# Gating the first weight load on the first scaled q, with a new written order for the opening of a gated linear attention and MLP kernel

## The chip, the cores and the metric

The kernel runs on one core of a Trainium2 chip. The time is the device time of one execution in microseconds (us); lower is better. A profiled execution also has a span, from the first to the last instruction of the program; its own time is a little longer.

## The reference

Two parts follow each other. The first is a gated linear recurrence for 4 batches of 8 heads, 768 tokens, 48 values a head. The second is a two-layer MLP with a tanh gelu, on the 3072 tokens that the first part yields.

```
for t in range(768):                                   # per batch and head
    state = alpha[t][:, None] * state + outer(k[t], v[t])   # 48 x 48
    y[t]  = q[t] @ state
x   = y as (3072 tokens, 384)
out = gelu_tanh(x @ w_in) @ w_out                      # 384 -> 2048 -> 384
```

Inputs and outputs are float32; products inside are taken in bf16 (sums of logarithms in f16), with float32 sums.

## The kernel before

**Tiling.** Tokens are cut into 6 chunks of 128. A *pair* is one chunk of two batches, so there are 12 pairs, numbered 0 to 11; pairs 0 and 1 are the first chunk, pair 2 is the third pair. Within a pair, the two batches are units 0 and 1. The recurrence of a chunk is done in closed form: the logarithm of alpha (`ln`, line 349 or 351, ScalarE) is summed along the tokens by products on TensorE (`cum`, lines 336 to 370), its exponentials `b`, `binv` and `bend` come from ScalarE (lines 391 and 397), q is scaled by `b` and k by `binv` (`qp` and `kp`, line 408, VectorE; q' is the scaled q), both are transposed by TensorE (`t`, line 418) and copied out of PSUM (`ev`, line 436, ScalarE or VectorE), multiplied with each other (`attn`, line 479), masked to a triangle (`mask`, line 486, VectorE), and multiplied with v (`y`, lines 533 and 536). `x` copies the result out (line 543), `tx` transposes it (line 550) and `xe` copies the transpose (line 554). The state that goes on to the next chunk comes from `kv` (line 496) and `st` (lines 518 and 521). Pairs 0 and 1 are loaded in a packed layout, so their k is transposed back (`t`, line 444, and a further `ev`, line 451) before `kv`. `vb` casts v of these pairs (line 379).

**MLP.** `l1` (line 562) is one of 8 steps of layer one for a pair, 6 products of 128x256, `gelu` (line 568) its gelu on ScalarE, `l2` (line 581) one of 4 steps of layer two for one unit, 4 products of 128x384; `ot` (line 593) copies a result and a store sends it. W_in and W_out are loaded in 4 parts each. A step `l1` of number 0 or 1 needs part 0 of W_in, 2 or 3 part 1, and so on. Layer two of pairs 0 and 1 is one block of 16 steps (`l20.0` to `l20.15`) ordered by part of W_out. PSUM banks come from three rings: `ff` (4 banks: layer one and two, products on zeros, early sums), `yk` (2 banks: transposes, y, kv) and `ca` (double, for sums and attn).

**Order.** Nothing orders the engines but a list of tasks that a small planner in the kernel file makes (`Scheduler.order`, lines 64 to 162). It first follows a list written out by hand or by search, `FIRST` (lines 184 to 196), whose entries read engine:step, with P for TensorE, V for VectorE, A for ScalarE, G for GpSimd (called POOL in the profile), S for SyncE. A step's name is its kind, its pair (for `l1`, `gelu` and `l2` its block) and a number: `qp0.1` is the scaled q of pair 0, unit 1. `fill.3` means three products on zeros, which do no work of the kernel. When the list is used up, a greedy rule goes on, by costs in a table `W` and by deps and free buffers. Each engine executes its own tasks in that order; semaphores do the rest. `LANDED` (line 197) tells the planner when the first loads are there; no instruction comes from it.

**Loads.** The first twelve loads (alpha, q and k of pairs 0 and 1, each by unit) are issued by SyncE. All others are issued by GpSimd in the order of `LOADS` (line 179): `v0` and `v1` are v of pairs 0 and 1, `in 0` the first part of W_in, `out 0` the first part of W_out, `2a` and `2b` the units of pair 2, a bare number a whole pair. An entry `gate` makes GpSimd copy one column of a named tile (line 304), so that all that GpSimd issues afterwards is held until that tile is there. Loads by GpSimd cast to bf16 on the way, except v of pairs 0 and 1.

Of the kernel before, what the change touches and what calls it, by code (L numbers as in the profile page):

```python
# [21 lines left out]
COST = {  # L22
    ("ACT", "b"): (385, 135), ("ACT", "binv"): (385, 135), ("ACT", "ev"): (600, 40), ("ACT", "gelu"): (510, 110),
    ("ACT", "ln"): (430, 140), ("ACT", "vb"): (420, 140), ("ACT", "x"): (370, 140), ("DVE", "end"): (110, 90),
    ("DVE", "ev"): (605, 115), ("DVE", "kp"): (480, 120), ("DVE", "mask"): (605, 115), ("DVE", "qp"): (480, 120),
    ("DVE", "st"): (470, 130), ("DVE", "x"): (480, 120), ("DVE", "xe"): (270, 120),
}
LAT = {"SP": 0, "PE": 210, "ACT": 110, "DVE": 90, "POOL": 0}
# [18 lines left out]
class Scheduler:  # L47
# [16 lines left out]
    def order(self):  # L64
        free = {e: 0 for e in LAT}
        taken = {tag: [] for tag in self.bufs}
        table, wire, xbar, head, out = LN_EXP, 0, 0, 0, []
# [26 lines left out]
        def put(t, at, e):  # L94
            nonlocal wire, xbar
            for tag, users in t.takes:
                taken[tag].append(users)
            cost, lat = COST.get((e, t.kind), (t.cost[e], LAT[e])) if fixed else (t.cost[e], LAT[e])
            t.start, t.end, t.engine, t.load = at, at + cost, e, None
            free[e] = t.end  # L100
            t.done = t.end + lat
            if t.name in self.landed:
                t.done = self.landed[t.name]
                if e != "SP":
                    wire = t.done - W["receipt"]
            elif t.land is not None:
                wire = max(wire, t.end + W["lead"]) + t.land
                t.done = wire + W["receipt_hw" if e == "SP" else "receipt"]
            if t.kind in ("turn", "store"):
                xbar = t.done = max(xbar, t.end + W["landed"] - t.xbar) + t.xbar  # L110
                t.done += t.late
            out.append(t)

        def go(at, e, t):
            nonlocal table, head
            if e == "PE" and not fixed and self.fill and at < self.until and at - free[e] > 300:
                g = given("ff")
                n = int((at - max(free[e], g if g is not None else at) - 60) * 0.95 // W["fill"])
                if n > 0:
                    f = Task("fill", {"PE": n * W["fill"]}, 0, self.fill(n))  # L120
                    put(f.take("ff", f), max(free[e], g), e)
            put(t, at, e)
            if t.table not in (None, table):
                table = t.load = t.table
            for q in t.cost:
                left[q].remove(t)
            if t.stream is not None:
                head = min((x.stream for x in left["PE"] if x.stream is not None), default=None)

        fixed = True  # L130
        for step in self.first:
            e, name = step.split(":")
            if name[:5] == "fill.":
                n = int(name[5:])
                f = Task("fill", {"PE": n * W["fill"]}, 0, self.fill(n))
                at = given("ff")
                assert at is not None, "no bank for idle products"
                put(f.take("ff", f), max(free["PE"], at), "PE")
                continue
            e, t = {"P": "PE", "V": "DVE", "A": "ACT", "G": "POOL", "S": "SP"}[e], self.named[name]  # L140
            at = ready(t, False)
            assert at is not None, f"{name} can't go yet"
            go(max(at, free[e] + (W["table"] if t.table not in (None, table) else 0)), e, t)
        fixed = False
        while any(left.values()):
            best = None
            for e in LAT:
# [7 lines left out]
                if found:  # L155
                    window = min(f[2] for f in found) + 60
                    at, t, _ = min((f for f in found if f[2] <= window), key=lambda f: (f[1].prio, f[0]))
# [14 lines left out]
class _Kernel:  # L172
# [3 lines left out]

    SPLIT = (2,)
    EARLY = (0, 1)
    LOADS = ('gatea 0 1', 'v0', 'gateqp 0 1', 'in 0', 'v1', 'in 1', 'in 2', 'in 3', 'out 0', 'out 1', '2a', 'out 2', '2b', 'out 3', '3', '4', '5', '6', '7', '8', '9', '10', '11')

    PACKED, CUM_FF, R = (0, 1), (0, 1), 4
    RINGS = (('a', 0, 0, 1), ('a', 0, 1, 2), ('q', 0, 0, 1), ('k', 0, 0, 1), ('q', 0, 1, 2), ('k', 0, 1, 2),
             ('a', 1, 0, 1), ('a', 1, 1, 2), ('q', 1, 0, 1), ('k', 1, 0, 1), ('q', 1, 1, 2), ('k', 1, 1, 2))
    FIRST = """
        A:table.0 S:load.0 S:load.1 S:load.2 S:load.3 S:load.4 A:ln0.0 S:load.5 P:fill.7 P:cum0.0 A:ln0.1 G:gate.0 G:load.12 S:load.6 P:cum0.1 A:b0.0 S:load.7
        A:binv0.0 V:qp0.0 A:bend0.0 A:b0.1 V:kp0.0 S:load.8 P:fill.2 P:t0.0 A:bend0.1 A:binv0.1 V:ev0.0 P:t0.1 S:load.9 A:ev0.1 S:load.10 V:qp0.1 P:fill.3
        P:attn0.0 V:kp0.1 P:t0.2 G:gate.1 S:load.11 G:load.13 V:mask0.1 P:fill.1 P:t0.3 G:load.14 A:ev0.3 V:end0.0 V:ev0.2 A:ln1.0 V:mask0.0 P:fill.4
        P:attn0.1 G:load.15 P:cum1.0 V:mask0.2 A:vb0.0 G:load.16 A:ln1.1 V:vb0.1 P:y0.0 V:mask0.3 A:b1.0 P:cum1.1 G:load.17 A:x0.0 V:qp1.0 A:binv1.0 P:y0.1
        G:load.18 A:b1.1 P:t1.0 V:x0.1 A:bend1.0 G:load.19 A:ev1.0 V:kp1.0 P:fill.2 P:tx0.1 V:xe0.1 A:binv1.1 P:tx0.0 G:load.20 P:t1.1 A:bend1.1 V:xe0.0
        G:load.21 V:qp1.1 P:t0.5 A:ev1.1 V:kp1.1 G:load.22 A:ev0.5 P:fill.1 P:attn1.0 G:load.23 P:t1.3 V:mask1.1 P:t1.2 A:ev1.3 P:l10.0 G:load.24 V:mask1.0  # L190
        A:ev1.2 P:kv0.1 G:load.25 V:end1.0 V:st0.1 P:t0.4 G:load.26 P:attn1.1 A:ev0.4 P:t1.5 G:load.27 A:ev1.5 V:vb1.0 G:load.28 V:mask1.2 P:y1.0 P:l10.1
        G:load.29 A:x1.0 V:mask1.3 A:vb1.1 P:kv0.0 P:tx1.0 G:load.30 V:st0.0 P:l10.3 V:xe1.0 P:y1.1 P:kv1.1 G:load.31 P:l10.2 V:x1.1 A:gelu0.0 V:st1.1 P:tx1.1
        A:gelu0.1 G:load.32 P:l10.4 V:xe1.1 A:gelu0.3 P:l10.5 A:gelu0.2 G:load.33 P:l11.0 A:gelu0.4 A:gelu0.5 P:l11.1 A:gelu1.0 P:l11.2 A:gelu1.1 P:l11.6
        A:gelu1.2 P:l10.6 A:gelu1.6 P:l11.5 A:gelu0.6 P:l11.7 A:gelu1.5 P:l11.4 A:gelu1.7 P:l10.7 A:gelu1.4 P:l11.3 A:gelu0.7 P:t1.4 A:gelu1.3 P:l20.1 V:ev1.4
        P:l20.2 P:kv1.0 P:l20.5
    """.split()
    LANDED = {"load.0": 2800, "load.1": 3400, "load.2": 4400, "load.3": 5100, "load.4": 6750, "load.5": 7300, "load.12": 9850, "load.6": 9000, "load.7":
              10300, "load.8": 10800, "load.9": 11300, "load.10": 11900, "load.11": 12300, "load.13": 14900, "load.14": 17600, "load.15":
              19300, "load.16": 21300, "load.17": 23000, "load.18": 25000, "load.19": 26600, "load.20": 27700, "load.21": 28400, "load.22":
              29000, "load.23": 29400, "load.24": 31300, "load.25": 32100, "load.26": 32700, "load.27": 33300, "load.28": 33800, "load.29":  # L200
              35900, "load.30": 37700, "load.31": 39400, "load.32": 41300, "load.33": 42600}

# [399 lines left out]
    def tasks(self):  # L602
        s = self.s = Scheduler(self.BUFS, self.fill, 60000, self.FIRST, self.LANDED)
        B, NCH = self.B, self.NCH
# [28 lines left out]
        for r, m, lo, hi in self.RINGS:  # L633
            loads[r, m, lo] = loads[r, m, hi - 1] = s.add(
                "load", {"SP": W["ring_issue"]}, n, self.load(r, *pairs[m], lo, hi), land=(W["ring_v" if r == "v" else "ring"] * (hi - lo) // 2 if n else W["begin"]))
            n += 1
        for step in self.LOADS:
            if step[0] == "v":
# [261 lines left out]
```

## Time and profile before

| | us |
|---|---|
| median of 6 runs | 178.77 |
| lowest, highest | 177.92, 180.44 |
| the profiled execution | 179.0 |
| its span | 177.2 |
| TensorE busy in the span | 171.9 |
| ScalarE busy | 130.7 |
| VectorE busy | 94.9 |

In a timeline line the columns are: start in us, length in us, engine, line of the kernel, operation, output<-input by the program's names, shapes, and the number of instructions merged; in brackets the idle time of the engine ahead of it and what ended it. PE is TensorE, PEld its weight loads, DVE VectorE, ACT ScalarE. Ends of products are modelled, so two products that overlap in the list follow each other at the distance of their starts. Merged lines name the first shape only.

### The profile page before, as it was taken

The page shows a single profiled execution, that of the slowest core. Times are in us where ns is not written, and L with a number is a line of the kernel's source. Part 1 is how long each engine was busy: PE and PEld are TensorE (multiplying, and loading weights), DVE is VectorE, ACT ScalarE, POOL GpSimd, SP SyncE. Part 2 cuts the span into 40 slices and gives each one's busy share as a digit, 9 for nine tenths or more (in the row PEclk, how much of TensorE's full clock was granted, in tenths as well). Part 3 has the DMA queues.
Part 4 walks back from the last instruction along what each step waited for, and adds up shares of the span by engine and source line. Part 5 has one row for each costly group of instructions (what it writes and reads, how often), then busy time and mean ns, then how long its engine had stood idle before and what let it go on. Part 6 is the DMA issues. An engine that isn't in the chain of part 4 may idle for free.

```text
span 177.2 us, 4413 instructions
## 1 busy us (share of the span) xinstructions
PE 171.9 (97%) x1831; PEld 136.0 (77%) x1833; DVE 94.9 (54%) x187; ACT 130.7 (74%) x216; POOL 57.8 (33%) x64
## 2 busy tenths in 40 slices
PE   7999999999999999999999999999999999999992
PEld 2666899666896897797698698688697697786972
DVE  6498820454967994696499797495426505000000
ACT  4658899785898668858788967977988884481831
POOL 2387437996735766667640000000000000000000
PEclk9999999999999999999999999999999999999999
DMA  4999999999999999999999992361270360401102
GB/s 118 293 259 188 203 231 234 233 238 198 240 286 196 228 263 215 196 256 205 197 249 234 198 190 55 65 175 41 46 209 4 89 162 5 131 1 48 44 3 86
DMA packets 48900, 28.86 MB, mean 163 GB/s; under 512 B 37488, under 2 KB 45296, under 8 KB 48880
## 3 DMA queue, kind: packets, MB, share of 16 engines
q0 software_dynamic: 26464, 17.70, 60.8%
q1 hardware_dynamic: 22416, 10.88, 24.8%
q8 instruction: 14, 0.23, 0.6%
q14 instruction: 6, 0.05, 0.1%
HBM read 25.17 MB, written 4.72 MB: 169 GB/s over the span
## 4 chain that ended last, share of the span: by engine, by line
PE 89%; DMA 6%; ACT 2%; issue 1%; DVE 1%; SPq 0%; POOL 0%
PE hT L562 36%; PE acc L581 35%; DMA v<-in_v_dram 4%; PE at L479 4%; PE qkT_ps L418 3%; PE yps L536 3%; PE kv L496 2%; DMA a<-in_alpha_dram 2%; PE yps L533 2%; PE cum L368 2%; PE xT_ps L550 1%; ACT qkT L436 1%; PE cum L370 1%; PE k_ps L444 1%; PE cum L336 0%
## 5 line engine op out<-in xcount | busy, mean ns | idle before, releaser
L581 PE MATMUL acc<-w_out,gT 128*128 128x384 bf16 (+1 forms) x400 | 69.4, 319 | 0.0
L562 PE MATMUL hT<-xT,w_in 128*128 128x256 bf16 x576 | 68.8, 273 | 0.0
L568 ACT ACTIVATE gT<-hT 128x512 bf16<-128x512 f32 x96 | 56.1, 599 | 15.1 <-PE hT L562 11.6
L562 PEld LDWEIGHTS <-w_in 128*128 128x128 bf16 x576 | 61.2, 114 | 1.5
L581 PEld LDWEIGHTS <-gT 128*128 128x128 bf16 x400 | 36.5, 97 | 18.9
L486 DVE TENSOR_TENSOR atm<-at,ut 128x512 bf16<-128x512 f32 x48 | 30.1, 681 | 13.9 <-PE at L479 13.9
L408 DVE TENSOR_TENSOR qp<-q,b 128x768 bf16<-128x768 f32 (+1 forms) x15 | 11.9, 796 | 17.8 <-ACT b L397 17.8
L593 ACT COPY ot<-acc 128x384 f32<-128x384 f32 (+1 forms) x18 | 8.3, 461 | 13.7 <-PE acc L581 11.5
L298 POOL DMA_DIRECT2D k<-in_k_dram x11 | 12.2, 1108 | 8.8 <-DMA vb<-in_v_dram 3.7
L298 POOL DMA_DIRECT2D q<-in_q_dram x11 | 12.2, 1108 | 6.0 <-DMA w_in<-in_moe_w_in_dram 1.0
L298 POOL DMA_DIRECT2D a<-in_alpha_dram x11 | 12.2, 1113 | 5.4 <-DMA w_in<-in_moe_w_in_dram 1.3
L298 POOL DMA_DIRECT2D vb<-in_v_dram x11 | 12.1, 1103 | 5.1 <-DMA a<-in_alpha_dram 1.3
L270 ACT ACT_TABLE_LOAD x9 | 11.5, 1283 | 0.9 <-PEq L884 0.7
L397 ACT ACTIVATE b<-cum 128x768 bf16<-128x768 f32 (+1 forms) x15 | 10.2, 682 | 2.3 <-PE cum L370 1.5
L408 DVE TENSOR_TENSOR kp<-k,binv 128x768 bf16<-128x768 f32 (+1 forms) x15 | 11.8, 790 | 0.0
L568 ACT ACT_TABLE_LOAD x9 | 11.5, 1283 | 0.2
L397 ACT ACTIVATE binv<-cum 128x768 bf16<-128x768 f32 (+1 forms) x15 | 10.2, 681 | 0.0
L518 DVE TENSOR_TENSOR stmp<-kv,st 128x384 f32<-128x384 f32 x16 | 8.8, 552 | 2.0 <-PE kv L496 2.0
L543 DVE CAST x<-yps 128x384 bf16<-128x384 f32 x12 | 6.7, 557 | 5.6 <-PE yps L536 5.5
L521 DVE TENSOR_TENSOR st<-stmp,ends 128x384 bf16<-128x384 f32 x16 | 8.9, 558 | 0.6
L351 ACT ACTIVATE la<-a 128x768 f16<-128x768 f32 (+1 forms) x11 | 8.5, 783 | 0.8 <-DMA a<-in_alpha_dram 0.7
L536 PE MATMUL yps<-vb,atm 128*128 128x48 bf16 x192 | 8.7, 183 | 0.2 <-ACT vb L379 0.2
(64 smaller groups left out, 156.0 us busy)
## 6 DMA issues: line engine op xcount, KB each, us to landing
out_dram<-ot SPq DMA_DIRECT2D x23, 192.0 KB, 2.4
a<-in_alpha_dram POOLq DMA_DIRECT2D x9, 384.0 KB, 11.7
q<-in_q_dram POOLq DMA_DIRECT2D x9, 384.0 KB, 11.7
k<-in_k_dram POOLq DMA_DIRECT2D x9, 384.0 KB, 11.5
vb<-in_v_dram POOLq DMA_DIRECT2D x9, 192.0 KB, 11.7
w_in<-in_moe_w_in_dram POOLq DMA_DIRECT2D x4, 384.0 KB, 9.5
w_out<-in_moe_w_out_dram POOLq DMA_DIRECT2D x4, 384.0 KB, 11.1
a<-in_alpha_dram SPq DMA_DIRECT2D x4, 192.0 KB, 3.8
```

Source lines behind the costliest of these rows:

```text
L270: nc.scalar.add_instruction(mybir.InstLoadActFuncSet(name=nc.get_next_instruction_name(), act_func_set_id=i, engine=mybir.EngineType.Activ ...
L298: dma(u[t][:, lo:hi].rearrange("t b h d -> t (b h) d"), src.rearrange("b h s d -> s (b h) d")[c * C:(c + 1) * C])
L351: self.nc.scalar.activation(u["la"][:, lo:hi, :, 0:self.D], u["a"][:, lo:hi], AF.Ln)
L397: self.nc.scalar.activation(u[n].rearrange("t i h d -> t i (h d)")[:, lo:hi], cum, AF.Exp, scale=1.0 if n == "b" else -1.0)
L408: self.nc.vector.tensor_tensor(out, rows, b, op=ALU.mult)
L486: self.nc.vector.tensor_tensor(u["atm", i][:, o], u["at", i][o], self.ut[:, None, :].to_broadcast([self.C, self.H // 2, self.C]), op=ALU.mult)
L518: nc.vector.tensor_tensor(s, acc, old, op=ALU.add)
L521: nc.vector.tensor_tensor(new.rearrange("f p (o d) -> f (p o) d", o=2), acc.rearrange("f p (o d) -> f (p o) d", o=2), ends, op=ALU.mult)
L536: nc.tensor.matmul(y[:, h, :], u["atm", i][:, h % 2, h // 2, :], u["vb"][:, i, h, :], start=c == 0, stop=True, skip_group_check=True)
L562: self.nc.tensor.matmul(h[:, s], w_in[:, j, nt % 4 + s], self.xT[c % self.NX][:, j, lo:hi].rearrange("p g t -> p (g t)"), start=j == 0, st ...
L568: return lambda e: self.nc.scalar.activation(self.gT[c % self.NG][:, nt:nt + 2, lo * self.C:hi * self.C], f.pop(("h", c, lo, nt)), AF.Gelu ...
L581: self.nc.tensor.matmul(f["acc", c, b][:, lo:hi], self.gT[c % self.NG][:, nt, b * self.C:(b + 1) * self.C], self.w_out[:, nt, lo:hi], star ...
```

## The change

Four things change, all of them in the order of the work; no instruction of the computation is added or left out, apart from products on zeros and one more gate.

1. `LOADS`: a second gate on q' of pair 0 is put in. Before, GpSimd issued v0, waited for `qp0.1` and then issued part 0 of W_in. Now it waits for `qp0.0`, issues part 0, then waits for `qp0.1`, and then goes on with v of pair 1.
2. `FIRST`: the list is made anew for all engines, and is longer. Before it ended at `l20.5`; now it ends at `l12.1`, the second step of layer one of the third pair. Engines change for several copies (for example `ev0.0`, `ev0.4`, `vb0.0`, `ot0.0`), `kv0.0`, `kv1.0` and some transposes stand earlier, `kv1.1` later, the steps of `l20` stand in another order, and the list's products on zeros are 16 instead of 20.
3. `LANDED`: the planner is given other landing times.
4. Line 98: while it follows the list, the planner prices the tasks of the fourth pair and later by the general table rather than by the measured one.

From the first step of layer two of the third pair (`l22.0`) on, TensorE's order is the same as before.

```diff
-            cost, lat = COST.get((e, t.kind), (t.cost[e], LAT[e])) if fixed else (t.cost[e], LAT[e])
+            cost, lat = COST.get((e, t.kind), (t.cost[e], LAT[e])) if fixed and not 300 <= t.prio < 10000 else (t.cost[e], LAT[e])
...
-    LOADS = ('gatea 0 1', 'v0', 'gateqp 0 1', 'in 0', 'v1', 'in 1', 'in 2', 'in 3', 'out 0', 'out 1', '2a', 'out 2', '2b', 'out 3', '3', '4', '5', '6', '7', '8', '9', '10', '11')
+    LOADS = ('gatea 0 1', 'v0', 'gateqp 0 0', 'in 0', 'gateqp 0 1', 'v1', 'in 1', 'in 2', 'in 3', 'out 0', 'out 1', '2a', 'out 2', '2b', 'out 3', '3', '4', '5', '6', '7', '8', '9', '10', '11')
...
     FIRST = """
         A:table.0 S:load.0 S:load.1 S:load.2 S:load.3 S:load.4 A:ln0.0 S:load.5 P:fill.7 P:cum0.0 A:ln0.1 G:gate.0 G:load.12 S:load.6 P:cum0.1 A:b0.0 S:load.7
-        A:binv0.0 V:qp0.0 A:bend0.0 A:b0.1 V:kp0.0 S:load.8 P:fill.2 P:t0.0 A:bend0.1 A:binv0.1 V:ev0.0 P:t0.1 S:load.9 A:ev0.1 S:load.10 V:qp0.1 P:fill.3
-        P:attn0.0 V:kp0.1 P:t0.2 G:gate.1 S:load.11 G:load.13 V:mask0.1 P:fill.1 P:t0.3 G:load.14 A:ev0.3 V:end0.0 V:ev0.2 A:ln1.0 V:mask0.0 P:fill.4
-        P:attn0.1 G:load.15 P:cum1.0 V:mask0.2 A:vb0.0 G:load.16 A:ln1.1 V:vb0.1 P:y0.0 V:mask0.3 A:b1.0 P:cum1.1 G:load.17 A:x0.0 V:qp1.0 A:binv1.0 P:y0.1
...
+        A:bend0.0 V:qp0.0 A:binv0.0 A:binv0.1 S:load.8 V:kp0.0 P:fill.2 P:t0.0 G:gate.1 G:load.13 A:b0.1 P:fill.1 P:t0.1 S:load.9 A:ev0.0 V:qp0.1 A:ev0.1
+        S:load.10 P:fill.2 P:t0.2 G:gate.2 G:load.14 V:kp0.1 A:bend0.1 P:attn0.0 S:load.11 V:ev0.2 P:t0.3 A:ev0.3 G:load.15 V:end0.0 V:mask0.1 P:fill.1 P:t0.4
+        P:t0.5 A:ln1.0 V:mask0.0 G:load.16 P:attn0.1 A:ev0.4 P:cum1.0 V:mask0.2 G:load.17 A:ev0.5 V:vb0.0 A:ln1.1 G:load.18 V:mask0.3 P:fill.2 P:kv0.0 A:b1.0
+        P:y0.0 P:cum1.1 G:load.19 V:st0.0 A:vb0.1 A:x0.0 V:qp1.0 P:y0.1 G:load.20 A:binv1.0 V:x0.1 P:t1.0 A:b1.1 G:load.21 V:kp1.0 A:ev1.0 P:fill.1 P:tx0.0
+        G:load.22 V:xe0.0 A:binv1.1 P:t1.1 V:qp1.1 G:load.23 P:tx0.1 A:ev1.1 V:xe0.1 G:load.24 V:kp1.1 A:bend1.0 P:attn1.0 A:bend1.1 G:load.25 P:t1.3 V:end1.0
+        V:mask1.1 P:t1.4 A:ev1.3 P:l10.0 G:load.26 V:ev1.4 G:load.27 P:t1.2 V:mask1.0 P:kv0.1 A:ev1.2 G:load.28 P:l10.1 V:vb1.0 G:load.29 V:st0.1 P:kv1.0
+        P:attn1.1 V:st1.0 P:t1.5 G:load.30 V:mask1.3 P:y1.0 A:gelu0.0 P:l10.2 V:mask1.2 A:ev1.5 G:load.31 P:l10.3 V:vb1.1 A:x1.0 A:gelu0.2 P:y1.1 G:load.32
+        P:tx1.0 P:l10.5 V:x1.1 A:gelu0.1 V:xe1.0 A:gelu0.3 P:tx1.1 P:l10.4 G:load.33 V:xe1.1 A:gelu0.5 P:l11.0 A:gelu0.4 P:l11.2 A:gelu1.0 P:l11.7 A:gelu1.2
...
+        A:gelu1.3 P:l20.2 P:l20.3 A:ln2.0 P:l20.6 P:cum2.0 P:l20.4 A:b2.0 A:binv2.0 P:l20.8 V:qp2.0 A:bend2.0 A:ln2.1 V:kp2.0 P:l20.10 V:st1.1 P:cum2.1 P:t2.0
+        A:bend2.1 A:binv2.1 P:l20.1 A:ev2.0 V:kp2.1 P:l20.5 A:b2.1 P:l20.9 V:qp2.1 P:attn2.0 P:t2.1 V:mask2.1 P:l20.12 A:ev2.1 V:mask2.0 P:l20.13 P:attn2.1
+        P:y2.0 V:mask2.3 P:l20.14 A:x2.0 V:mask2.2 A:ln3.0 P:l20.7 P:y2.1 P:tx2.0 P:cum3.0 V:x2.1 V:xe2.0 P:l20.11 V:ot0.0 A:ot0.1 A:ot0.2 A:b3.0 P:tx2.1
+        P:l20.15 S:store0.0 A:bend3.0 S:store0.1 V:xe2.1 S:store0.2 A:binv3.0 V:qp3.0 P:kv2.0 P:kv2.1 P:l12.0 V:ot0.3 P:l12.1
     """.split()
```

## The prediction

> **What bounds the kernel now.** I read the page's busy line first, then the chain that ended last.
>
> ```profile
> PE 171.9 (97%) x1831; PEld 136.0 (77%) x1833; DVE 94.9 (54%) x187; ACT 130.7 (74%) x216; POOL 57.8 (33%) x64
> ...
> PE 89%; DMA 6%; ACT 2%; issue 1%; DVE 1%; SPq 0%; POOL 0%
> ```
>
> TensorE is the bound, and its 97% flatters it: products on zeros (`fill`) count as busy. So I cut the span where the order of the work turns (columns: stretch, length, busy us and count of PE, PEld, DVE, ACT, POOL, clock, DMA share, GB/s), and then took line 279, the products on zeros, alone (PE and PEld only).
>
> ```profile
> 7.08:17.18 10.10, 9.33 (x121) 6.08 (x121) 8.98 (x19) 7.08 (x19) 6.81 (x10) 1.00 1.05 240
> 17.18:22.69 5.51, 5.35 (x77) 4.66 (x75) 4.95 (x11) 4.94 (x9) 2.43 (x3) 1.00 1.22 202
> 22.69:45.80 23.11, 23.11 (x235) 17.89 (x235) 8.06 (x18) 18.43 (x34) 17.34 (x17) 1.00 1.26 227
> ...
> 52.94:172.20 119.26, 119.26 (x1275) 95.90 (x1273) 64.06 (x111) 89.66 (x138) 25.28 (x22) 1.00 0.76 138
> ```
>
> ```profile
> 7.08:17.18 10.10, 3.22 (x11) 1.05 (x13) 1.00 1.05 240
> ```
>
> From 22.69 us on PE never stops; before that it does. The timeline gives start-to-start prices of real steps where they stand back to back: a layer-1 step 0.655 us (12 of them from 22.69 to 30.55), a layer-2 step 0.65, a packed `cum` 0.76, an early `t` 0.223, an early `attn` 0.33, `kv` 0.17, an early `y` 0.18, `tx` 0.165. Counting the steps of each stretch with these: 7.08 to 17.18 holds 5.20 us of real work and **4.90 lost**; 17.18 to 22.69 holds 4.60 and **0.92 lost**; 22.69 to 52.94, where both orders join, loses 0.54 (0.22 of it the `fill` before `kv2.0` at 45.25). The 6.36 us lost after the first two `cum` is all that a new order can win. The timeline tells what ends the two early stretches:
>
> ```profile
> 9.27 0.36 POOL L304 CAST gate<-qp 128x1 f32<-128x1 bf16 x1 [2.72 <-DVE qp L408]
> 9.74 0.75 POOL L311 DMA_DIRECT2D w_in<-in_moe_w_in_dram  x1
> ...
> 11.79 0.51 ACT L379 CAST vb<-v 128x384 bf16<-128x384 f32 x1 [0.70 <-DMA v<-in_v_dram]
> ...
> 16.39 0.40 PE L479 MATMUL at<-qkT 64*128 64x128 bf16 x8 [0.18 <-ACT qkT L436]
> ...
> 17.18 0.82 PE L562 MATMUL hT<-xT,w_in 128*128 128x256 bf16 x6
> ...
> 22.69 8.02 PE L562 MATMUL hT<-xT,w_in 128*128 128x256 bf16 x72
> ```
>
> Issue plus time to landing (DMA view, one issue at a time) gives v0 5.26 + 6.5 = 11.76, W_in part 0 9.74 + 6.9 = 16.67, part 1 20.57, part 2 22.46. So part 0 is not what the first layer-1 step waits for: it landed 0.5 us earlier. Part 2 is what `l10.4` at 22.69 waited for, and part 1 lands 0.05 us before `l10.3`.
>
> **What the Trainium skill says.** *DMA: Bandwidth & Descriptors*, "Queues, rings and completion order": each DMA engine takes its queues in turn, packet by packet. The trace agrees: from 8 us on, while POOL's v0 moves, SP's q and k loads of pair 1 go on, and they take 5.5 to 6.0 us to land against 3.0 for the first load. So an earlier W_in part 0 does share with those loads. *TensorE: Matmul & The Clock Gate*, "Why this matters for your kernels": no idle gap over about 3 us, or the clock halves. The granted clock is 1.00 in every stretch; the trace shows no such gap after 1.2 us. *ScalarE: Activation LUTs*, "What ACT_TABLE_LOAD costs": 1283 ns plus about 1380 ns of drain. The trace has the 1283, and no drain: the load starts at 20.75, the first gelu at 22.05.
>
> **The change, part by part.** The new text of prices (line 98) only moves the planner's clock; no instruction costs more or less for it.
>
> *The gate.* `qp0.0` ends at 6.95; the gate's copy takes 0.36; so part 0 is issued near 7.4 instead of 9.74, 2.3 us sooner. `gate.2` then waits for `qp0.1` (about 8.7, below); v1, parts 1 to 3 and W_out queue behind it on POOL and are issued near 9.2, 10.4, 11.1, 11.9 and 12.6, each some 1.25 us sooner. POOL has no other work that anyone waits for, so the extra gate costs 0. What does it win? Part 0 itself nothing (slack 0.5). Parts 1 and 2 stand in one queue behind part 0 and v1, and land sooner only by what the DMA engines leave unused meanwhile:
>
> ```profile
> 12.00:13.00 1.00, 0.75 (x15) 0.53 (x14) 1.00 (x3) 1.00 (x4) 1.00 (x2) 1.00 0.98 184
> ...
> 15.00:16.00 1.00, 0.83 (x12) 0.62 (x9) 1.00 (x4) 0.49 (x3) 0.95 (x2) 1.00 0.91 228
> ...
> 20.00:21.00 1.00, 1.00 (x15) 0.92 (x13) 0.75 (x2) 0.98 (x3) 0.14 (x1) 1.00 1.26 208
> ```
>
> Against 1.24 (the mean of 18 to 21 us), 12 to 18 us run at 0.98, 1.15, 1.16, 0.91, 1.07, 1.13: short by 1.04, or 0.84 us of transfer. Bounds for parts 1 and 2: 0 to 0.84 us sooner; I take 0.5.
>
> *The first pair.* `b0.1` moves behind `binv0.1` on ACT, so `qp0.1` starts at 7.25 + 0.38 + 0.38 + 0.14 = 8.15; all copies of the first transposes but one go to ACT (0.59 us each, DVE 0.69). `attn0.0` is then ready at about 9.25, 0.4 later than now, with `t0.2` ahead of it. This is covered by v0: its cast `vb0.0` moves to DVE behind `mask0.2`, near 12.1, and v0 lands at 11.76, slack 0.3. Then DVE has, start to start, `vb0.0` 0.32, `mask0.3` 0.61, `st0.0` 0.47, `qp1.0` 0.48, `x0.1` 0.48, `kp1.0` 0.5: about 15.0. Hand-off 0.2, `t1.1` at 15.3, ACT's copy 15.7 to 16.3, **`attn1.0` at 16.4, as now (16.39)**, and the first layer-1 step at 17.2, as now. But by then `t0.4` (0.22) and `kv0.0` (0.17) are done too: **0.39 won**. Nine products on zeros stand where thirteen stood; they cost nothing, as PE waits there anyway.
>
> *17 to 22 us.* `kv1.0` and one transpose's copy (`ev1.4`, now DVE's) come here, which now stand at 30.6 to 32.4; DVE is full from 16.9: `mask1.1`, `ev1.4`, `mask1.0` (0.61 each), `vb1.0` 0.32, two `st` 0.47 each, so 20.0. `y1.0` needs the bank that the second `st` frees: 20.1. Then `l10.2`, `l10.3`, `y1.1`, `tx1.0`: 20.3 + 2 x 0.655 + 0.18 + 0.165 = **21.97 for the first step on part 2**. It lands at 22.46 now and PE follows 0.23 later; half a microsecond sooner makes that 22.2. So 22.69 - 22.2 = **0.5**, and the work done by then is larger by 0.06 (`t1.4` 0.22 and `kv1.0` 0.17 in, `tx1.1` 0.165 and `kv1.1` 0.17 out). The 0.39 above is part of this 0.56, not beside it. ACT puts `gelu0.0` with its table load ahead of `ev1.5` and `x1.0`; `gelu0.0` could start near 18.3 and starts at 20.2, so that cover is 1.9 us.
>
> *22.7 to 53 us.* Same steps in another order, PE full. The `fill` before `kv2.0` goes (0.22), and three of four hand-offs of 0.095 before `attn`; `t2.1` may wait 0.15 for `qp2.1`, whose `b2.1` ACT now takes after a copy of 1.01 us. Loads land at least 0.9 us before use here (W_out part 2 at 32.75, used near 33.8). **Won: 0.3.** From 52.94 on both orders are the same and every later load lands over 6 us ahead of use.
>
> *Sum.* 0.5 + 0.06 + 0.3 = 0.86, taken as 0.85. The profiled execution took 179.0 us, 177.2 of it span; so 178.15 for such a run. It lies 0.2 over the median of 178.77, which becomes **177.9**.
>
> **Rivals.** (A) *W_in gains nothing*: DMA shares of 0.9 to 1.16 speak for it, being near full. Part 2 at 22.46, start at 22.69: only 0.06 + 0.3, so **178.4**. (B) *The early chain shortens too*: the DVE chain above is a sum of spacings; if v1, q and k come as needed and copies on ACT end sooner, `l10.0` moves to about 16.4 and `y1.0` follows; with parts 1 and 2 at 0.84 sooner another 0.8: **177.1**. Against it: DVE is 8.98 of 10.10 busy. (C) *Slower, the landing of v0*: part 0 takes turns with v0 and with q and k of pair 1. Slack of v0 is 0.3 us, of q and k 1.2 to 1.6; past it each microsecond moves `y0.0`, `qp1.0` and all behind by one. From v0 1.2 us later than now (12.95) the gain is gone; at 13.8 it is **179.6**. For it: these loads already take 6 us. Against it: v0's packets stand before part 0's in POOL's own queue. Slower by 1% needs v0 at 14.7. (D) *The change does not reach its aim*, PE's clock drops with fewer products on zeros: half speed for some 3.4 us, +1.7, **179.7**; no gap in the new order exceeds 0.7 us.
>
> **How the numbers follow.** Forecast 0.57, A 0.15, B 0.14, C 0.11, D 0.03. The bounds of the landings give 177.7 to 178.4 alone; runs of the kernel itself scatter from 177.92 to 180.44. Range 176.9 to 179.3: it leaves out the lower part of B and the upper parts of C and D. One per cent, about what a measurement can tell from no change, is 1.8 us: faster by that 0.13 (most of B), slower by that 0.07 (the end of C, D), within it 0.80.
>
> **What would show it.** Right: W_in part 0 issued near 7.4; `attn1.0` still near 16.4; the long run of layer-1 steps begins near 22; no product on zeros near 45; `l22.0` near 52.1; the rest shifted whole. Wrong: v0's cast after 12.2 (C); the first step on part 2 still at 22.7 (A); `l10.0` before 16.8 (B); a clock under 1 between 8 and 20 us (D).

## The result, and the profile after

Over 29 executions the changed kernel's median is 181.72 us; the kernel before, run 66 times beside it on the same chips, has 178.56. That median hides two groups. Ten of the 29 lie between 177.46 and 179.35 (median 178.19), nineteen between 180.18 and 184.32. Of the kernel before, none of the 66 lies over 180.44. The ratios in this document leave out executions more than 1.5% over the fastest of the same kernel, here the whole upper group: 0.998, with a 95% interval of 0.996 to 1.000, no difference that can be measured. But the upper group is not noise from outside: the sections below trace it to the early gate.

The first profile of the changed kernel fell in the upper group: 182.89 us, 181.1 of it span. The page's busy line, the clock in 40 slices and the chain that ended last, by engine (in the new kernel's code each line has a number higher by 3 than before: 565 is layer one, 584 layer two, 411 the scaled q and k):

```profile
PE 171.8 (95%) x1826; PEld 136.2 (75%) x1828; DVE 95.0 (52%) x188; ACT 130.4 (72%) x215; POOL 58.2 (32%) x65
...
PEclk9998589999999999999999999999999999999999
...
PE 87%; DMA 6%; SPq 4%; issue 0%; DVE 0%; ACT 0%; DVEq 0%
```

TensorE is as busy as before; the chain now runs for a tenth of the span through one load of k (6%) and SyncE's issues (4%), and the clock falls to half for a stretch near 20 us. The timeline of this profile shows the place:

```profile
7.56 0.75 POOL L314 DMA_DIRECT2D w_in<-in_moe_w_in_dram  x1
...
8.29 0.89 SPq L298 DMA_DIRECT2D k<-in_k_dram  x1
...
15.95 0.40 PE L482 MATMUL at<-qkT 64*128 64x128 bf16 x8 [0.44 <-ACT qkT L439]
...
19.43 0.56 DVE L411 TENSOR_TENSOR kp<-k,binv 128x384 bf16<-128x384 f32 x1 [3.36 <-DMA k<-in_k_dram]
...
20.05 0.61 PE L421 MATMUL qkT_ps<-ident,kp 128*128 128x128 bf16 x4 [3.70 <-DVE kp L411]
...
20.88 1.48 PE L565 MATMUL hT<-xT,w_in 128*128 128x256 bf16 x6
```

The gate did its work: part 0 of W_in is issued at 7.56. `attn1.0` stands at 15.95. But `kp1.1`, the scaled k of pair 1, unit 1, waits for the last of SyncE's twelve loads (issued at 8.29, landed at 19.3; in the kernel before issued at 8.15, landed at 13.68), and TensorE waits for `kp1.1`. So the first layer-1 step starts at 20.88. The DMA view of this one load, in the kernel before and here (the last column is us to landing):

```profile
k<-in_k_dram SPq DMA_DIRECT2D x1, 192.0 KB, 5.5
...
k<-in_k_dram SPq DMA_DIRECT2D x1, 192.0 KB, 11.0
```

The same kernel was profiled again, and that execution (177.56 us, span 175.8) belongs to the lower group. TensorE is 96% of its chain. Its timeline at the same places:

```profile
7.51 0.75 POOL L314 DMA_DIRECT2D w_in<-in_moe_w_in_dram  x1
...
15.91 0.40 PE L482 MATMUL at<-qkT 64*128 64x128 bf16 x8 [0.44 <-ACT qkT L439]
...
16.84 0.82 PE L565 MATMUL hT<-xT,w_in 128*128 128x256 bf16 x6
...
21.51 0.82 PE L565 MATMUL hT<-xT,w_in 128*128 128x256 bf16 x6
```

Here k landed at 15.21, just in time, and `l10.0` starts at 16.84. The step at 21.51 is `l10.5`, in the new order the first on part 2 of W_in; it waits for nothing. The stretches of both profiles (columns: stretch, length, busy us and count of PE, PEld, DVE, ACT, POOL, clock, DMA share, GB/s), first the late one:

```profile
13.00:17.18 4.18, 2.47 (x40) 1.76 (x39) 2.82 (x7) 2.80 (x8) 2.55 (x4) 0.97 1.16 260
17.18:22.69 5.51, 2.64 (x20) 2.25 (x21) 2.53 (x6) 0.59 (x1) 1.76 (x2) 0.50 1.22 210
22.69:27.00 4.31, 4.31 (x60) 3.69 (x59) 2.68 (x6) 4.15 (x7) 1.74 (x3) 0.87 1.11 242
```

```profile
7.08:16.84 9.76, 8.79 (x121) 5.83 (x120) 8.87 (x20) 7.95 (x21) 7.83 (x11) 1.00 1.12 269
16.84:22.33 5.49, 5.49 (x79) 5.08 (x77) 4.80 (x11) 4.95 (x9) 2.32 (x3) 1.00 1.21 210
```

The late execution has 20 matmuls where the kernel before has 77, at half the clock. The two profiles of the same program are 5.33 us apart: 4.04 of it is there when `l10.0` starts (20.88 against 16.84), the remaining 1.3 comes while the clock is still at half.

The DMA view tells who got the engines. Columns: queue, packets, MB, busy time as a share of 16 engines. `q1` is the hardware queue, here SyncE's loads; `q0` is the software queue, GpSimd's loads. First the late profile at 9 to 11 us (SyncE's queue), then at 15 to 17 and 17 to 19.4:

```profile
q1 hardware_dynamic: 562, 0.41, 74.4%
...
q0 software_dynamic: 297, 0.40, 103.4%
q1 hardware_dynamic: 54, 0.04, 8.6%
...
q0 software_dynamic: 488, 0.48, 121.0%
q1 hardware_dynamic: 13, 0.01, 1.7%
```

the profile of the lower group at 9 to 11 and 15 to 17, and last the kernel before at 9 to 11:

```profile
q1 hardware_dynamic: 885, 0.64, 98.1%
...
q0 software_dynamic: 375, 0.39, 116.9%
...
q1 hardware_dynamic: 639, 0.47, 77.2%
```

In the late execution SyncE's loads are behind already at 9 to 11 us (562 packets against 885), but that alone is no sign: the kernel before had 639 there, and its k landed at 13.68. The last 67 packets of the late execution, 0.05 MB, then take from 15 to 19.3 us beside 785 of GpSimd's. In its trace no two of SyncE's packets are under way together after 17.3 us, and the last six of data start 0.124 us apart; in the second late profile below it is the last thirteen. That looks like a single DMA engine with part of the load still to move, the other engines being done with it; the trace does not name the engines.

### The profile page after: what moved, and what is told of

It reads as the page before. It is cut to its first block, busy times and chain, and to the rows that moved or that the text cites. A ratio compares the mean times of both kernels' runs of the same rounds, so it can differ in the third digit from the quotient of the medians.

```text
span 181.1 us, 4401 instructions
## 1 busy us (share of the span) xinstructions
PE 171.8 (95%) x1826; PEld 136.2 (75%) x1828; DVE 95.0 (52%) x188; ACT 130.4 (72%) x215; POOL 58.2 (32%) x65
## 4 chain that ended last, share of the span: by engine, by line
PE 87%; DMA 6%; SPq 4%; issue 0%; DVE 0%; ACT 0%; DVEq 0%
PE hT L565 36%; PE acc L584 35%; DMA k<-in_k_dram 6%; SPq L298 4%; PE at L482 3%; PE qkT_ps L421 3%; PE yps L539 2%; PE kv L499 2%; PE yps L536 2%; PE cum L371 2%; PE xT_ps L553 1%; PE cum L373 1%; PE k_ps L447 0%; DVE kp L411 0%; ACT ot L596 0%
## 5 line engine op out<-in xcount | busy, mean ns | idle before, releaser
L565 PE MATMUL hT<-xT,w_in 128*128 128x256 bf16 x576 | 70.0, 275 | 0.0
L571 ACT ACTIVATE gT<-hT 128x512 bf16<-128x512 f32 x96 | 56.8, 599 | 15.9 <-PE hT L565 12.3
L596 ACT COPY ot<-acc 128x384 f32<-128x384 f32 (+1 forms) x17 | 7.7, 460 | 13.2 <-PE acc L584 12.4
L439 ACT COPY qkT<-qkT_ps 128x512 bf16<-128x512 bf16 (+1 forms) x10 | 7.0, 717 | 8.6 <-PE qkT_ps L421 8.5
L400 ACT ACTIVATE binv<-cum 128x768 bf16<-128x768 f32 (+1 forms) x15 | 10.2, 681 | 0.3 <-PE cum L343 0.3
L421 PE MATMUL qkT_ps<-ident,kp 128*128 128x128 bf16 x56 | 5.7, 226 | 3.8 <-DVE kp L411 3.7
```

The source lines that it names most:

```text
L400: self.nc.scalar.activation(u[n].rearrange("t i h d -> t i (h d)")[:, lo:hi], cum, AF.Exp, scale=1.0 if n == "b" else -1.0)
L421: nc.tensor.transpose(ps[:, j, p, :], u[n + "p"][:, i, 2 * p:2 * p + 2, :].rearrange("t h d -> t (h d)"), self.ident)
L565: self.nc.tensor.matmul(h[:, s], w_in[:, j, nt % 4 + s], self.xT[c % self.NX][:, j, lo:hi].rearrange("p g t -> p (g t)"), start=j == 0, st ...
L571: return lambda e: self.nc.scalar.activation(self.gT[c % self.NG][:, nt:nt + 2, lo * self.C:hi * self.C], f.pop(("h", c, lo, nt)), AF.Gelu ...
L596: self.copy(e)(f["ot", c, b][:, sl], f["acc", c, b] if half is None else f["acc", c, b, half][:, sl])
```

## The experiments

The theory after the first profile: W_in's part 0, issued ahead of SyncE's last loads, delays them; TensorE's pause then drops the clock. The rival: the new order does it, and the gate is innocent. A second rival: v1 and the later parts of W_in, which stand closer behind part 0 now, do it. "Late" below counts executions with a mean clock under 0.995, which is how the profiled late ones look (0.98 to 0.991). It is a sign only: when k landed is known for the profiled executions alone. Of the kernel before, no execution beside these runs is late.

### The changed kernel again, and profiled once more

Neither differs from the changed kernel.

> The changed kernel once more, for a second profile. In its first profile the last load of SyncE's ring, k of pair 1 unit 1, landed at 19.34 us (13.68 before), kp1.1 stood at 19.43 instead of 15.94, PE idled 3.7 us and its clock fell to half from 17 to 23 us. Theory G (the earlier gate does it: W_in part 0 and what follows it take turns with SyncE's q and k loads): the landing moves from execution to execution, anywhere from 14 to 20 us; where it is before about 16 us the time is 177.5 to 178.5, else 180 to 184. Rival O (the new order does it, with fewer products on zeros): attn1.0 late and the clock low whatever the landing.

> The changed kernel once more, to see an execution in which the last k load is in time. Then: attn1.0 near 15.9, the first layer-1 step near 16.8, W_in parts 1 and 2 at 20.0 and 21.9 or earlier and the first step on part 2 right behind, l22.0 0.9 to 1.3 sooner than before. If the load is late again, as in the two profiles so far: kp1.1 waits for it, PE idles over 2 us.

Measured: in the first, 9 executions with a median of 181.84, seven of them late; the two others give a ratio of 0.9945 (0.9917 to 0.9972). Its profile (184.38) has part 0 issued at 7.08 and three loads late: k of unit 0 at 14.94, q of unit 1 at 18.89, k of unit 1 at 21.01. (This k of unit 0 was issued at 6.81, ahead of part 0.) The second is the 177.56 shown above. So the two groups come back, about two in three late: 25 of 39 in all.

### The new order with the old gate

```diff
-'v0', 'gateqp 0 0', 'in 0', 'gateqp 0 1', 'v1',
+'v0', 'gateqp 0 1', 'in 0', 'v1',
-P:t0.0 G:gate.1 G:load.13 A:b0.1 ... P:t0.2 G:gate.2 G:load.14
+P:t0.0 A:b0.1 ... P:t0.2 G:gate.1 G:load.13 G:load.14
```

> The new order of the engines, but W_in part 0 gated on qp0.1 as before (one gate, parts 1 to 3 right behind v1). Theory G: k of pair 1 unit 1 lands near 13.7 to 14.5 again, no stretch with a clock below 1.00, all executions 177.6 to 178.4, ratio 0.993 to 0.999. Rival O: as the changed kernel, median about 181, clock down near 17 us.

Measured: median 178.05 of 20, one of them late; ratio 0.9966 (0.9950 to 0.9983). TensorE's order is that of the changed kernel, so the order is not what makes k late. Without the early gate it meets W_in instead. From this kernel's timeline:

```profile
19.86 1.50 PE L565 MATMUL hT<-xT,w_in 128*128 128x256 bf16 x12 [0.20 <-DMA w_in<-in_moe_w_in_dram]
...
21.75 0.26 PEld L565 LDWEIGHTS <-w_in 128*128 128x128 bf16 x3 [0.19 <-DMA w_in<-in_moe_w_in_dram]
```

`l10.2` waits for part 1 (19.81) and `l10.5` for part 2 (21.71). `l22.0` starts at 51.75, 1.19 sooner than before.

### The new gate with the old order

```diff
-'v0', 'gateqp 0 1', 'in 0', 'v1',
+'v0', 'gateqp 0 0', 'in 0', 'gateqp 0 1', 'v1',
-V:kp0.0 S:load.8 P:fill.2 ... P:t0.2 G:gate.1 S:load.11 G:load.13
+V:kp0.0 S:load.8 G:gate.1 G:load.13 P:fill.2 ... P:t0.2 G:gate.2 S:load.11
```

> The old order of the engines with the new gate alone: part 0 is issued after qp0.0, near 7.4 us, and the rest after qp0.1 (8.57 us start in the old order), 0.4 later than in the changed kernel. Theory G: the last k load lands late (15 to 20 us) in a good part of the executions, kp1.1 and attn1.1 wait for it, 178.5 to 182. Rival O: like before, 178.3 to 179, the load at about 13.7.

Measured: 184.19, 182.13, 180.38, 179.65, the first two late; ratio without the first 1.0118 (1.0047 to 1.0189). Beside them 28 executions of the kernel before took at most 179.20. The profile (184.19) has part 0 issued at 7.39, and

```profile
19.44 0.56 DVE L408 TENSOR_TENSOR kp<-k,binv 128x384 bf16<-128x384 f32 x1 [1.39 <-DMA k<-in_k_dram]
...
20.05 0.61 PE L418 MATMUL qkT_ps<-ident,kp 128*128 128x128 bf16 x4 [2.79 <-DVE kp L408]
```

The gate alone does it, with the old order of all other engines. The first rival falls.

### Part 0 early, all behind it held until q' of pair 1

```diff
-'in 0', 'gateqp 0 1', 'v1',
+'in 0', 'gateqp 1 0', 'v1',
```

In the list, GpSimd's entries behind part 0 move to behind `qp1.0`; no other engine's do.

> The changed kernel with W_in part 0 still gated on qp0.0, but v1 and all that GpSimd issues after it held until qp1.0 (about 13.1 to 13.7 us) instead of qp0.1; engine orders as in the changed kernel. Theory G1 (part 0 alone, in the queues ahead of SyncE's last two loads, delays them): the last k load still lands past 16 us in many executions, median 180 to 182. Theory G2 (v1 and parts 1 to 3 behind it do it): it lands by 15, all executions about 178 to 179.5, with W_in part 1 landing near 20.5 and part 2 near 22.3.

Measured: 182.77 to 184.99, median 183.35; ratio 1.029 (1.0245 to 1.0335). Three of four are late by the clock. In the profile, which is not, SyncE's last load landed at 14.68, 1.2 us later than with the old gate (13.47), though GpSimd had issued nothing behind part 0. So part 0 alone delays k. That it alone makes k late is not shown: k was in time in this profile, and the low clock of the other three may come from a wait at 102 us (below). With that wait removed, the same opening gave four executions, none of them late, and k landed at 15.4 in the one profiled (pair 11's loads held back, below); at the changed kernel's rate of 25 in 39, four in a row without a late one would come about once in sixty. So the second rival does not fall: v1 and the later parts of W_in may well be what makes a delay of 1 to 2 us into one of 5 and more. Most of the loss here was something else, which no theory had expected. `l22.0` starts at 52.75, 0.19 sooner than before; the time goes at 102 to 106 us. From the timeline:

```profile
94.31 1.33 SPq L465 DMA_TRANSPOSE xT<-x  x1
...
97.70 4.55 SPq L465 DMA_TRANSPOSE xT<-x  x1
...
105.94 0.82 PE L565 MATMUL hT<-xT,w_in 128*128 128x256 bf16 x6 [3.77 <-DMA xT<-x]
```

and from the DMA view of the first of these issues alone (the last column is us to landing):

```profile
xT<-x SPq DMA_TRANSPOSE x1, 10.2
```

`l16.0`, layer one of pair 6, takes its x from two DMA transposes that SyncE issues near 94 and 98 us. They landed at 104.49 and 105.89, when GpSimd's last load was in (104.63). I compared the kernels so far and those that follow (the wait is counted from start to start):

```
                         last load   first transpose   l16.0    its wait
kernel before              100.14       100.50         102.19     none
changed, 177.56             98.30        98.67         100.73     none
new order, old gate         99.65       100.00         101.27     0.27
rest held                  104.63       104.49         105.94     3.9
gate on k' (below)          99.87       100.16         101.49     0.19
two issues moved (below)    99.09        99.44         101.18     none
both (below)               101.93       101.79         103.27     2.4
```

In all of them the first transpose lands within 0.4 us of the last load. The end of GpSimd's stream of loads sets how soon `l16.0` can run; in the kernel before, `l16.0` came 0.4 us after its second transpose (101.79).

### Part 0 later, and part 0 with no gate

```diff
-'v0', 'gateqp 0 0', 'in 0', 'gateqp 0 1', 'v1',
+'v0', 'gatekp 0 1', 'in 0', 'v1',             (first kernel)
+'v0', 'in 0', 'gateqp 0 1', 'v1',             (second kernel)
```

> The new order with W_in part 0 gated on kp0.1 (about 9.1 us), so part 0 is issued near 9.5, 0.6 later than with the gate on qp0.1 and 1.9 later than in the changed kernel. Theory G (what counts is whether part 0 enters the queues before SyncE's last load is issued at 8.2 to 8.8): the last k load lands by 14 in every execution, all times 177.3 to 178.8, median 178.0, ratio 0.995 to 0.998; parts 1 and 2 land some 0.2 to 0.4 later than with qp0.1. Rival O (the order, fewer products on zeros): one in ten executions over 180 as with qp0.1.

> The new order with no gate ahead of W_in part 0: it is issued right behind v0, near 5.9 us, before SyncE's loads 8 to 11; the rest after qp0.1 as in the changed kernel. Theory G: several of SyncE's last loads land late, at the least k of unit 0 and q and k of unit 1; every execution over 180, the last k load past 17. Rival (only the last load is ever late, whatever the gate): as the changed kernel, median 181.8 with some at 177.5.

Measured: later, 178.53 of 14, none late; ratio 1.0008 (0.9991 to 1.0025), so the gain that was expected (0.995 to 0.998) did not come. v1 lands at 18.39 and `kv1.0` starts 0.76 late for it. With no gate, 182.22 and 182.34, both late; ratio 1.0215 (1.0173 to 1.0257). There part 0 is issued at 5.87 and SyncE's last five loads all land late; ScalarE or VectorE waits for four of them; three of these waits:

```profile
12.67 0.52 ACT L352 ACTIVATE la<-a 128x384 f16<-128x384 f32 x1 [1.01 <-DMA a<-in_alpha_dram]
14.60 0.56 DVE L411 TENSOR_TENSOR qp<-q,b 128x384 bf16<-128x384 f32 x1 [1.48 <-DMA q<-in_q_dram]
...
19.00 0.56 DVE L411 TENSOR_TENSOR kp<-k,binv 128x384 bf16<-128x384 f32 x1 [1.17 <-DMA k<-in_k_dram]
```

The sooner part 0 is issued, the more loads are late. Standing ahead of part 0 is no full cover: this alpha was issued at 5.46, 0.4 us before part 0, and took 7.2 us (4.1 in the kernel before). In the second late profile k of unit 0 had a lead of 0.3 us and took 8.1, and with the new gate on the old order a lead of 0.6 and took 8.0; in the kernel before this k took 5.9.

### SyncE's last load ahead of part 0: two issues moved to ScalarE

If what counts is how far part 0 is ahead of SyncE's last issue, that can be turned around without giving up the early gate: SyncE issues its loads one after the other, 0.65 us each; here ScalarE takes two of them, ahead of its first table load.

```diff
-A:table.0 S:load.0 S:load.1 S:load.2 S:load.3 S:load.4
+A:load.1 A:table.0 S:load.0 S:load.2 A:load.3 S:load.4
-            dma = (nc.sync if e == "SP" else nc.gpsimd).dma_start
+            dma = {"SP": nc.sync, "ACT": nc.scalar}.get(e, nc.gpsimd).dma_start
-                "load", {"SP": W["ring_issue"]}, n,
+                "load", {"ACT" if n in (1, 3) else "SP": W["ring_issue"]}, n,
```

> The changed kernel, but two of SyncE's first loads (alpha of unit 1 and k of unit 0 of pair 0) are issued by ScalarE, around its first table load, where it idles. SyncE's list is two issues (1.3 us) shorter, so its last load is issued at about 6.9 to 7.5 us, before W_in part 0 (7.4 to 7.6). Theory G, in its strict form (a SyncE load is late only if part 0 enters the queues before it is issued): the last k load lands by 14 in nearly all executions, times 177.2 to 178.0, median 177.6, ratio 0.993 to 0.997. Rival S (part 0 shares the engines with whatever of pair 1 is still unmoved at 9 us, whenever that was issued): late as often as before, median 181 to 182.

Measured: median 177.61 of 22 (177.16 to 179.39), none late and none over 180; ratio 0.9949 (0.9931 to 0.9967). In the profile (177.98) the last k is issued at 7.22 and landed at 13.54; part 0, its gate now at 7.62, is issued at 8.09:

```profile
7.22 0.96 SPq L298 DMA_DIRECT2D k<-in_k_dram  x1
...
8.09 0.75 POOL L314 DMA_DIRECT2D w_in<-in_moe_w_in_dram  x1
```

From 17.29 to 22.69 TensorE is busy for 5.40 of 5.40 us, as in the lower group of the changed kernel. This version has the lowest median of all here, ahead of the kernel before and of the changed kernel. Part 0 itself is issued 0.5 us later here than in the changed kernel, so the run does not tell its place behind k from its time.

The same two issues moved, with the old gate (new order):

```diff
-'v0', 'gateqp 0 0', 'in 0', 'gateqp 0 1', 'v1',
+'v0', 'gateqp 0 1', 'in 0', 'v1',
```

> As the kernel before it in this call, but with part 0 gated on qp0.1 (issued near 8.9). Theory G: no late landing at all (two of twenty executions had one without the move to ScalarE), median 177.9 to 178.1, ratio 0.996 to 0.998: GpSimd's loads end near 99.6 us as with the old gate, so the first step of layer one on DMA-transposed rows at 101 waits a little, as it did there. Rival S: one in ten late, median the same.

Measured: 178.03 of 22, none late; ratio 0.9968 (0.9953 to 0.9984). The early gate is thus worth 0.4 us here, and the two intervals overlap. The profile drawn is this kernel's slowest execution (180.07), and shows the wait at `l16.0` again, 2.4 us. And the two issues moved in the kernel before, with the new gate (old order):

```diff
-'v0', 'gateqp 0 1', 'in 0', 'v1',
+'v0', 'gateqp 0 0', 'in 0', 'gateqp 0 1', 'v1',
```

> The old order of the engines with the new gate and with the two first loads issued by ScalarE, to see what the gate is worth on the old order once SyncE's last loads are not in its way. Theory G and E: k of pair 1 unit 1 lands by 14 in nine of ten executions; W_in part 2 lands near 21.6 instead of 22.46, so the long run of layer one begins 0.4 to 0.8 us sooner; with the loads ending a microsecond sooner nothing waits at 101: 177.9 to 178.4, ratio 0.996 to 0.999. Rival (the gate wins only together with the new order): 178.4 to 178.8, ratio about 1.

Measured: 178.84 of 14, one late; ratio 1.0024 (0.9997 to 1.0051), where the forecast was 177.9 to 178.4 and its rival had 178.4 to 178.8. In the profile the first step on part 2 comes at 22.34 instead of 22.69 and `l22.0` at 52.58 instead of 52.94. So on the old order the gate wins 0.35 us of one profile, and nothing that the median shows.

All kernels by the time from SyncE's last issue to part 0's (both in the profiles):

```
                              last k issued   part 0 issued   late executions
no gate                           8.22            5.87            2 of 2
changed kernel, three profiles    8.12-8.63       7.08-7.56      25 of 39
old order, new gate               8.39            7.39            2 of 4
rest held                         8.20            7.35            3 of 4
  with pair 11 held               8.10            7.50            0 of 4
new order, old gate               8.16            8.87            1 of 20
gate on k'                        8.12            9.05            0 of 14
two issues moved                  7.22            8.09            0 of 22
  with pair 11 held               7.09            8.00            2 of 20
  with the old gate               7.18            9.15            0 of 22
  with the old order              7.30            7.91            1 of 14
```

Part 0 ahead of the last k: 32 of 53, or 29 of 45 without the kernels that hold the rest, whose clock is no safe sign. Behind it: 4 of 112. All four are among those with a lead of 0.6 to 0.9 us, so such a lead makes it rare and not impossible; that holds for the best version too, which with and without pair 11's loads held has 2 late in 42. In the same table part 0 is issued before 7.6 us where k is often late and after 7.9 where it is rarely, so its place and its time go together, and no run parts them. A smaller delay of k need not lower the mean clock this far, and isn't counted: eight more of the 112 took over 180 at full clock (four of them with pair 11 held). One of the eight was profiled, the 180.07 above, and its k was in time.

### Pair 11's loads held back

If the end of the load stream holds up the transposes at 94 us, holding the last pair's four loads until later must free them.

```diff
-'9', '10', '11')
+'9', '10', 'gatekp 8 0', '11')
```

> The kernel that held v1 and all behind it until qp1.0 (181.0 us of span, of which TensorE waited 3.9 us ahead of l16.0 for a transposed x), with one more gate: the four loads of pair 11 are held until kp8.0, about 101 us. Orders of TensorE, ScalarE and VectorE unchanged. Theory E (a DMA transpose issued at 94 us lands only when the loads queued before it have): turn6.0 lands near 97 instead of 104.5, l16.0 does not wait, 179.0 to 180.0 in all, unless the four loads push later transposes back. Rival (the transposes are slow for another reason): turn6.0 near 104 and 183 us as before.

> The kernel with two of the first loads issued by ScalarE, with the same gate ahead of pair 11. Theory E: turn6.0 lands near 95.5 instead of 99.4; there was no wait for it in the profile, so the median stays at 177.4 to 177.7, and the few executions at 179.3 go. Rival: the held loads get into the way of the transposes at 107 to 118 us, 178 to 179.

Measured, on the kernel with the rest held: 180.73 of 4 (180.45 to 180.87) against 183.35 without this gate; ratio to the kernel before 1.0113 (1.0085 to 1.0142). None of the four is late. The same transpose, issued at 94.92, now lands 2.4 us later instead of 10.2, and `l16.0` waits for nothing. So the load stream is what held the transpose. But the four loads, issued at 103.6 to 107.1, now stand in the way of the transposes of pairs 7 and 8:

```profile
117.90 0.85 PE L565 MATMUL hT<-xT,w_in 128*128 128x256 bf16 x6 [0.97 <-DMA xT<-x]
```

On the kernel with the two issues moved, which had no wait at `l16.0`, it only costs: 179.19 of 20 where 177.4 to 177.7 was expected, ratio 1.0054 (1.0032 to 1.0075), with `l17.0` 1.2 us late in the profile. Four more took 180.6 to 180.9 at full clock, and two were late.

## Why the prediction was right, and where it was wrong

The median of all executions, 181.72, lies 2.4 us over the range. The lower group's, 178.19, lies 0.3 over the forecast of 177.9, with its quickest five at 177.46 to 177.94. The prediction described one third of the executions well and gave the case that names the mechanism of the other two thirds, rival C, a chance of 0.11.

**The gate: right in time and in place.** Part 0 near 7.4: 7.56, 7.51. The parts behind it were to be issued near 9.2 (v1) and 10.4: 9.17 and 10.35. Nobody waited for GpSimd itself.

**What the gate wins: a term too small.** I let parts 1 and 2 land 0 to 0.84 us sooner, "only by what the DMA engines leave unused", and took 0.5. In the lower group's profile they landed at 18.43 and 20.31, 2.1 us sooner; in the late one part 1 landed at 20.75, no sooner than before, and with two issues moved to ScalarE they came 0.9 us sooner. So the size depends on the execution, and in the good one it was four times mine. I had taken a share of busy time for a rate. In the DMA view above SyncE's loads move 0.64 MB in 2 us at a share of 0.98, GpSimd's 0.39 MB at 1.17: 0.65 MB per full share against 0.33. The view counts a part of W_in as the 384 KB of bf16 that are written, where 768 KB of float32 are read, so by bytes read the two are about the same. (Of GpSimd's loads only W_in, W_out and v from pair 2 on are cast; alpha, q and k land as float32, contrary to the text ahead of the prediction.) A share of 0.9 to 1.16 thus did not say how much more could be moved. From 7.08 to 17.18 the kernel before moved 2.42 MB (10.10 us at 240 GB/s); this execution moved 2.63 by 16.84 (9.76 at 269).

**The first pair: right, half a microsecond too late.** `attn1.0` was to stay at 16.4 and stands at 15.91; `l10.0` at 16.84 instead of 17.2, so a part of rival B came true. v0, rival C's victim, was no trouble: it landed at 10.5 in this profile and 11.2 in the late one, against 11.76. It was also issued at 4.65 and 4.51 there, against 5.26, ahead of anything that the change touches; so part of the half microsecond may be the scatter of single executions.

**17 to 22 us: right in kind.** The forecast for the first step on part 2 was 22.2, bound by the weights, 21.97 if they were there. It is 21.51, the weights there and the chain 0.46 sooner: 1.18 won against 22.69, where the forecast had 0.5.

**22.7 to 53 us: right.** `l22.0` starts at 51.48 against 52.94, so 1.46 in all; that leaves 0.28 for the work done sooner and the hand-offs, where I had 0.06 + 0.3. The products on zeros near 45 are gone. So the sum was 0.85 and these two profiles show 1.46; the profile of before was itself 0.4 over its median, and the medians of what is not late say 0.4 (changed, lower group) to 1.0 (two issues moved, 177.61 against 178.60).

**Rival C: the right mechanism, the wrong load and a price far too low.** "Part 0 takes turns with v0 and with q and k of pair 1" is what happens; I gave q and k a slack of 1.2 to 1.6 us, priced the case by v0 coming up to 2 us late, 179.6, and saw 1% slower as its far end. What the traces show is a load whose last 67 packets go through in 4 us, and a landing 1.5 to 7.3 us later than before. This k had 2.3 us of slack in the kernel before (landed at 13.68, used at 15.94); its delay is the term that was far too small, as I priced a delay for v0 alone. The Trainium skill, *DMA: Bandwidth & Descriptors*, "Queues, rings and completion order", has each DMA engine take turns between its queues. The 67 packets against 785 do not contradict it, as they are counts over all 16 engines; one packet of SyncE's every 0.124 us at the end fits turns on an engine that still has both kinds of load.

**Rival D: an effect, not a cause of its own.** I said no gap in the new order would exceed 0.7 us. That holds in the lower group (clock 1.00 throughout). In the first late profile TensorE waits 3.7 us, the clock is at half from 17.0 to 23.8, and 1.3 us come on top of the 4.0.

**"Every later load lands over 6 us ahead of use": wrong as an argument.** True for loads, but it was meant to say that nothing after `l22.0` depends on the load stream. The DMA transposes do. In the kernel before the margin was 0.4 us, so any order that gains more than that in the first half runs into it, unless the load stream ends sooner too. The new order with the old gate gains 1.19 up to `l22.0` and keeps 0.92 at `l16.0`. With the early gate as well the stream ends at 98.30 instead of 99.65 (100.14 before), and this second benefit was not in my sum.

**What stays open.** The same program has k late in two executions of three and not in the third. In the late profiles SyncE's last issue takes 0.67 to 0.89 us, in the good one 0.62, but with two issues moved it took 0.96 and k was in time; what decides it, I have not found. Nor do the runs say whether part 0 alone can make k late, or whether its place behind k or its time of issue is what helps.

## What to carry to other kernels

Before a weight load is moved forward, list every load that the start of the kernel waits for, with its time of issue: here those issued after the weight load, or less than about 0.6 us ahead of it, were the ones that came late, and with 0.6 to 0.9 us of lead it was rare. Shortening the issuing queue (two issues on an idle engine) bought that lead. Look at all single times, not only at a median or at a ratio that leaves some out: a change can be neutral in one execution and cost 4 us in the next. And when the front of a kernel gets faster, list everything later that shares the DMA queues, transposes as well as loads, with its margin in the old profile.

## What the runs showed of the hardware that I had not expected

- A load of 192 KB took 5.5 us from issue to landing in the kernel before, and 10.7 to 12.4 in the four late profiles, where a casting load of 384 KB had been issued ahead of it; in three others with the same order of issue it took 6.5 to 7.3.
- A DMA transpose issued at 93 to 95 us, while loads were queued, landed within 0.4 us of the last of them in the seven profiles of the table: 6.0 us after its issue in the kernel before, 10.2 at most, 2.4 when the loads were held back. It is no general rule: behind the four held loads one issued at 108.74 landed 6.5 us later, at 115.2, and the last of these loads at 118.2.
- TensorE's clock does not go by the gap alone. The Trainium skill, *TensorE: Matmul & The Clock Gate*, "Why this matters for your kernels", names an idle gap of over about 3 us. Here the half clock came with a wait of 3.70 us, but also with 2.79 (the gate on the old order) and 1.87 (no gate; it came half a microsecond after this wait was over), each after some 4 us in which TensorE was 60% busy (2.53 of 4.20 us, 2.83 of 4.70). Where the wait was 3.70 us, TensorE had been 74% busy (2.43 of 3.30 us), and the clock fell 0.6 us into it. The half clock lasted 6.8 us there and 3.4 with no gate. What else the clock goes by, these runs do not show. After a full stretch (5.00 of 5.00 us) it stayed at 1.00 through a wait of 3.77 us and beyond (rest held, stretches around `l16.0`).

```profile
102.00:105.90 3.90, 0.17 (x2) 0.11 (x1) 0.84 (x3) 0.46 (x1) 0.00 (x0) 1.00 1.03 128
105.90:109.00 3.10, 3.06 (x43) 2.75 (x43) 1.97 (x4) 1.76 (x3) 0.00 (x0) 1.00 1.53 180
```
